# A sparse attention feeding a mixture of attention experts: one written order of 2573 operations replaced by another

## The chip, the cores and the metric

The kernel runs on one core of one Trainium2 chip. The metric is the device time of one execution in microseconds (us), from the start of the program to its end; lower is better. The profile's span runs from the first to the last instruction of the program, and is a little shorter than the time.

## What is computed

The input is `q`, `k`, `v` for 8 batches, 8 heads, 576 positions and 64 values a head, and the weights of four experts. Stage one is attention under fixed sparse masks; stage two sends its result through four causal attention experts, of which each position keeps the two with the largest gates.

```python
# stage one, a head: the first four heads see the last 32 positions, the others every 32nd
mask_local   = (rel >= 0) & (rel < 32)
mask_strided = (rel >= 0) & (pos[None, :] % 32 == pos[:, None] % 32)
x = softmax(where(mask, q @ k.T / 8, -1e9)) @ v            # heads side by side: 576 x 512
# stage two, expert e of four
logits = x @ w_gate                                        # weights w: softmax over the two largest
a  = softmax(where(causal, -1e9, (x @ wq[e]) @ (x @ wk[e]).T / 8))
ye = a @ (x @ wv[e]) @ wo[e]
out += mask[..., None] * w[:, :, kk:kk+1] * ye             # 8 x 576 x 512, float32
```

## The kernel before

The work is cut into 2573 small operations. The kernel first only notes them: `op(...)` stores what an operation does, the engine or the two engines that can do it, the tiles that it reads and writes and, for TensorE, the shape of the array that it uses (`mode`: the full 128 x 128 array, two halves of 64 rows, two of 64 columns, quarters of 64 x 64, and strips of 64 x 32 or 32 x 64). Nothing is issued until `schedule()` walks a list of numbers written into the kernel, `ORDER`, and issues the operations in that order. Each engine executes its own in the order of the list, and engines wait for each other only through the data and the buffers. So the list is the order of five queues at once: the four engines' and that of SyncE, which issues every DMA. `SECOND` names the operations that are done by the second of their two engines, and `FILL` the warming matmuls.

Buffers come from rings. The eight PSUM banks (ring `bank`, one of the tiles printed as `bank`) take every product; `nat` (3) holds `q` and `k` as loaded, `v1` (2) values, `th` (4) transposed weights, `ys` (3) output tiles. An operation that is the first to use a buffer asks its ring for one at its place in the list, and gets the free one whose last use stands furthest back in the list. In execution it then waits until that last use is over.

A fill is issued only `if o.fill and RB.first() is not None`: where no bank is free at that place of the list, none is made. Each fill is a 128 x 128 matmul of the identity into a free bank, whose result nobody reads; in float32 that is two matmul instructions.

`stage1(b, hp)` does two heads of one batch: loads (`load_qk`, `load_v`), transposes of `q` and `k` (`tp`, on TensorE in batches 0 and 1, else `tq` on VectorE), scores (`sl`, L628, for local heads, `s`, L642, for strided ones), mask, softmax over VectorE, GpSimd and ScalarE, a transpose of the weights (`pt`, L706, or on VectorE), values (`xal`, L736, or `xa`, L755), and a split of the result into a rounded part and its remainder (`xh`, `xl`). The local scores are 80 matmuls of 32 columns an operation, local values 84.

Stage two for a batch: `project` makes queries and keys of two experts at a time (`pj`, 12 matmuls, L906; for batch 0's first pair in parts of 3, L918), `values2` values and gates (`vp`, L853), `attend` the causal scores (`s2`, L992, and `s2_4`, L972), their softmax, transposes (`t2`, L1048, copied by `t2_out`), and the values (`acc`, L1081); `out_tile` makes 128 rows of output (`yp`, 6 matmuls, L1110), copies them (`yp_out`) and stores them. The copies `tp_out`, `pt_out`, `vp_out`, `t2_out` and `yp_out` can be done by ScalarE or VectorE; they share L338. `load_weights` loads the experts' weights and splits them (`hi_w`, `lo_w`).

Of the kernel before, what the change touches and what calls it, by code (L numbers as in the profile page):

```python
# [20 lines left out]
def attention_moe_kernel(  # L21
# [59 lines left out]
    class Ring:  # L81
# [24 lines left out]
        10, 11, 14, 15, 48, 52, 55, 58, 85, 86, 91, 111, 120, 121, 125, 146, 155, 159, 162, 165, 168, 171, 174,  # L106
        180, 185, 194, 197, 200, 210, 214, 215, 238, 247, 248, 249, 252, 253, 275, 310, 313, 314, 335, 336, 401,
        434, 468, 500, 501, 533, 534, 545, 566, 567, 578, 599, 632, 665, 666, 698, 722, 765, 798, 842, 855, 863,
        896, 897, 929, 963, 974, 995, 1029, 1086, 1106, 1127, 1161, 1269, 1353, 1355, 1356, 1375, 1406, 1426,
        1443, 1444, 1478, 1485, 1494, 1497, 1513, 1597, 1615, 1617, 1630, 1632, 1634, 1711, 1737, 1778, 1784,  # L110
        1802, 1836, 1852, 1855, 1877, 1920, 1924, 1974, 1990, 1992, 2038, 2097, 2119, 2122, 2123, 2126, 2142,
        2166, 2187, 2188, 2190, 2191, 2210, 2231, 2233, 2235, 2281, 2282, 2332, 2341, 2343, 2346, 2348, 2350,
        2396, 2399, 2427, 2429, 2449, 2453, 2455, 2477, 2483, 2491, 2494, 2518, 2520, 2524, 2548, 2559,
    }
    ORDER = [
        1, 0, 2, 44, 8, 45, 3, 13, 12, 5, 88, 15, 87, 56, 10, 7, 51, 6, 4, 9, 46, 49, 11, 16, 14, 18, 53, 55,
        47, 52, 57, 58, 48, 122, 54, 89, 19, 123, 21, 17, 201, 23, 202, 59, 50, 20, 25, 157, 90, 92, 22, 24,
        240, 93, 26, 27, 91, 28, 29, 61, 62, 64, 63, 65, 31, 94, 30, 96, 66, 239, 68, 127, 97, 129, 32, 67, 124,
        98, 99, 100, 128, 69, 33, 126, 40, 125, 36, 131, 213, 71, 70, 72, 203, 34, 60, 169, 132, 207, 37, 205,
        134, 208, 35, 172, 277, 215, 102, 278, 101, 41, 209, 308, 133, 135, 210, 73, 214, 307, 74, 103, 105,  # L120
        136, 104, 138, 75, 212, 38, 137, 251, 106, 252, 95, 39, 204, 76, 107, 211, 139, 206, 246, 81, 109, 83,
# [134 lines left out]
    ]  # L256
    FILL = {
        8: 4, 13: 1, 56: 2, 76: 2, 96: 6, 127: 2, 213: 1, 241: 3, 251: 8, 1131: 1, 1136: 1, 1137: 1, 1138: 5,
        1143: 1, 1144: 4, 1149: 4, 1150: 6,
    }  # L260

    def op(kind, eng, key, fn, r=(), w=(), mode=None, dmas=(), after=()):
# [931 lines left out]
```

## Time and profile before

| | us |
|---|---|
| median of 3 runs | 445.7 |
| lowest and highest run | 442.08, 446.44 |
| the profiled execution, its time | 446.46 |
| the profiled execution, its span | 444.7 |
| TensorE busy | 427.8 |
| VectorE busy | 345.9 |
| ScalarE busy | 269.5 |
| GpSimd busy | 221.0 |

The mean granted clock of TensorE over the span is 0.992 of full speed. The profile is of one execution. A page gives sums over the span; the timeline, the stretches and the chain of waits give places. The profile names engines PE (TensorE's matmuls), PEld (its weight loads, which overlap the matmuls), DVE (VectorE), ACT (ScalarE), POOL (GpSimd) and SP (SyncE). A matmul's end is modelled, so neighbouring matmuls overlap in these rows.

### The profile page before, as it was taken

The page shows a single profiled execution, that of the slowest core. Times are in us where ns is not written, and L with a number is a line of the kernel's source. Part 1 is how long each engine was busy: PE and PEld are TensorE (multiplying, and loading weights), DVE is VectorE, ACT ScalarE, POOL GpSimd, SP SyncE. Part 2 cuts the span into 40 slices and gives each one's busy share as a digit, 9 for nine tenths or more (in the row PEclk, how much of TensorE's full clock was granted, in tenths as well). Part 3 has the DMA queues.
Part 4 walks back from the last instruction along what each step waited for, and adds up shares of the span by engine and source line. Part 5 has one row for each costly group of instructions (what it writes and reads, how often), then busy time and mean ns, then how long its engine had stood idle before and what let it go on. Part 6 is the DMA issues. An engine that isn't in the chain of part 4 may idle for free.

```text
span 444.7 us, 19093 instructions
## 1 busy us (share of the span) xinstructions
PE 427.8 (96%) x7716; PEld 382.8 (86%) x7716; DVE 345.9 (78%) x1104; ACT 269.5 (61%) x848; POOL 221.0 (50%) x408
## 2 busy tenths in 40 slices
PE   7899998999989999999999999999999999999996
PEld 6788987977879998997889898998879998998874
DVE  6878899889985977789997768796998868555651
ACT  4475537676675757556486475557565577645662
POOL 4556641777534633376536552346833754405440
PEclk9989999999999999999999999999999999999999
DMA  6756656636545604545625336215832211001113
GB/s 178 188 140 151 126 116 125 125 58 107 113 103 118 124 23 105 113 90 118 117 50 131 68 59 124 61 33 107 193 76 73 67 43 54 1 1 58 45 68 118
DMA packets 156272, 41.89 MB, mean 94 GB/s; under 512 B 145976, under 2 KB 149432, under 8 KB 156184
## 3 DMA queue, kind: packets, MB, share of 16 engines
q1 hardware_dynamic: 156184, 40.67, 41.3%
q8 instruction: 61, 1.00, 0.9%
q14 instruction: 27, 0.22, 0.2%
HBM read 31.20 MB, written 9.44 MB: 91 GB/s over the span
## 4 chain that ended last, share of the span: by engine, by line
PE 85%; DVE 4%; SPq 3%; issue 3%; DMA 2%; ACT 2%; POOL 1%; POOLq 0%; DVEq 0%; ACTq 0%
PE bank L906 20%; PE bank L1110 12%; PE bank L853 10%; PE bank L1081 9%; PE bank L992 7%; PE bank L1048 6%; PE bank L736 4%; PE bank L972 3%; PE bank L755 3%; PE bank L628 3%; PE bank L642 3%; DMA v<-in_v_dram 1%; PE bank L706 1%; PE bank L816 1%; SPq L549 1%
## 5 line engine op out<-in xcount | busy, mean ns | idle before, releaser
L1029 POOL TENSOR_SCALAR p<-p,st,wt 128x512 f32<-128x512 f32 (+3 forms) x128 | 76.6, 610 | 42.4 <-DVE st L1013 17.2
L1004 ACT ACTIVATE p<-p,st 128x384 f32<-128x384 f32 (+3 forms) x128 | 71.8, 569 | 0.7 <-DVE st L999 0.6
L999 DVE CUSTOM_DVE_ANT_0 p<-bank,m_cau 128x128 f32<-128x128 f32 (+3 forms) x128 | 57.2, 481 | 6.6 <-PE bank L992 5.7
L927 ACT CAST qk<-bank 128x288 fp32r<-128x288 f32 x64 | 25.2, 400 | 56.3 <-PE bank L906 49.8
L338 ACT COPY th<-bank 128x384 f32<-128x384 f32 (+2 forms) x119 | 46.1, 436 | 13.5 <-PE bank L1048 9.8
L523 DVE STREAM_TRANSPOSE qkt<-nat 128x576 f32<-128x576 f32 x48 | 47.7, 1006 | 1.5 <-DMA nat<-in_k_dram 1.2
L1081 PE MATMUL bank<-th,vs 128*64 128x192 f32 (+4 forms) x512 | 48.5, 337 | 0.0
L1081 PEld LDWEIGHTS bank<-th,vs 128*64 128x64 f32 x512 | 33.6, 137 | 13.9 <-issue 6.9
L718 ACT CAST xh<-bank 128x128 fp32r<-128x128 f32 (+4 forms) x112 | 28.7, 322 | 21.6 <-PE bank L736 10.4
L720 DVE TENSOR_TENSOR xl<-bank,xh 128x128 fp32r<-128x128 f32 (+4 forms) x112 | 32.1, 324 | 12.4 <-ACT xh L718 11.7
L929 DVE TENSOR_TENSOR qkl<-bank,qk 128x288 fp32r<-128x288 f32 x64 | 27.8, 444 | 12.6 <-ACT qk L927 12.5
L1048 PE MATMUL bank<-ident,p 64*128 64x64 f32 x800 | 36.5, 226 | 0.5 <-DVE xl L720 0.3
L853 PE MATMUL bank<-wl_v,xh 128*128 128x260 f32 x128 | 36.2, 283 | 0.6 <-issue 0.6
L1048 PEld LDWEIGHTS bank<-ident,p 64*128 64x128 f32 x800 | 32.3, 139 | 5.3 <-issue 1.6
L853 PE MATMUL bank<-wh_v,xh 128*128 128x260 f32 x128 | 36.4, 284 | 0.0
L853 PE MATMUL bank<-wh_v,xl 128*128 128x260 f32 x128 | 36.2, 283 | 0.0
L906 PE MATMUL bank<-xh,wh_k 128*128 128x288 f32 x120 | 36.1, 301 | 0.0
L906 PE MATMUL bank<-xh,wh_q 128*128 128x288 f32 x120 | 35.9, 299 | 0.0
L906 PE MATMUL bank<-xl,wh_k 128*128 128x288 f32 x120 | 35.8, 299 | 0.0
L906 PE MATMUL bank<-xh,wl_k 128*128 128x288 f32 x120 | 35.8, 298 | 0.0
L906 PE MATMUL bank<-xl,wh_q 128*128 128x288 f32 x120 | 35.7, 298 | 0.0
L906 PE MATMUL bank<-xh,wl_q 128*128 128x288 f32 x120 | 35.5, 296 | 0.0
(182 smaller groups left out, 1254.4 us busy)
## 6 DMA issues: line engine op xcount, KB each, us to landing
out_dram<-ys SPq DMA_DIRECT2D x32, 256.0 KB
nat<-in_q_dram SPq DMA_DIRECT2D x96, 72.0 KB
nat<-in_k_dram SPq DMA_DIRECT2D x96, 72.0 KB
v<-in_v_dram SPq DMA_DIRECT2D x96, 40.0 KB
v<-in_v_dram SPq DMA_DIRECT2D x48, 54.0 KB
v<-in_v_dram SPq DMA_DIRECT2D x32, 48.0 KB
v<-in_v_dram SPq DMA_DIRECT2D x32, 45.0 KB
out_dram<-ys SPq DMA_DIRECT2D x8, 128.0 KB
```

The lines of the kernel that those rows point to most:

```text
L338: (nc.scalar.copy if e == "ACT" else nc.vector.tensor_copy)(dst, src)
L523: op("tq", {"DVE": 0.66 if local else 1.11}, k0 - 13, lambda e, x=x: nc.vector.transpose(turned(qkt.t, x), raw(x) if local else raw(x).rea ...
L720: op("xl", {"DVE": dve(n_)}, key + 0.5, lambda e, s_=s_, x_=x_: nc.vector.tensor_sub(x_(xl.t), s_(xa.t), x_(f(xh.t))), r=[xa, xh[u]], w=[x ...
L853: nc.tensor.matmul(vp.t[:, :NV], xx.t[:, t0:t0 + 128], ww.t[:, kt, :], start=i == 0, stop=i == 11)
L906: nc.tensor.matmul(pj.t[:, :HS], ww.t[:, kt, ep * 128:(ep + 1) * 128], xx.t[:, c], start=i == 0, stop=i == 11)
L992: nc.tensor.matmul(sp[a].t[:, :nk], x.t[r, 0, q0:q0 + 128], y.t[r, 1, :nk], start=i == 0, stop=i == 2)
L999: lambda e, sp=sp, p=p, a=a, nk=nk, ci=ci: nc.vector.tensor_tensor_reduce(out=p.t[:, a, :nk], in0=sp[a].t[:, :nk], in1=m_cau[:, S - nk:], ...
L1004: op("exp2", {"ACT": 0.285 + 0.00084 * nk}, k_ + 1, lambda e, p=p, a=a, ci=ci, nk=nk: nc.scalar.activation(p.t[:, a, :nk], p.t[:, a, :nk], ...
L1029: lambda e, p=p, a=a, ci=ci, t=t, nk=nk: nc.gpsimd.tensor_scalar(p.t[:, a, :nk], p.t[:, a, :nk], st.t[:, 20 + ci + a:21 + ci + a], wt.t[:, ...
L1048: nc.tensor.transpose(tp[hf].t[:, 64 * c:64 * c + 64], src, ident[r, r])
L1081: nc.tensor.matmul(acc.t[o, c0:c0 + cn], vw, th[a].t[:, s0:s0 + cn], start=j == 0, stop=j == idx[-1], skip_group_check=True)
L1110: nc.tensor.matmul(yp.t[:, :DM], xx.t[:, c0:c0 + 128], ww.t[:, ep, :], start=i == 0, stop=i == 5)
```

## The change

The three tables are replaced: `ORDER`, `SECOND` and `FILL`. The operations themselves, the rings and the tiles are the same. `ORDER` holds the same 2573 numbers in another order. `SECOND` has 165 members instead of 150, so that VectorE has 805 of the operations instead of 788, ScalarE 685 instead of 703, GpSimd 314 instead of 313; 461 on TensorE and 308 on SyncE are as before. `FILL` asks for 60 warming matmuls at 15 places instead of 52 at 17. In making the new list, an operation that asked for a buffer late was pushed behind the operation that releases it.

```diff
     SECOND = {
-        10, 11, 14, 15, 48, 52, 55, 58, 85, 86, 91, 111, 120, 121, 125, 146, 155, 159, 162, 165, 168, 171, 174,
...
+        6, 7, 10, 12, 42, 48, 49, 50, 54, 55, 86, 112, 120, 128, 146, 147, 155, 156, 168, 174, 180, 185, 188,
...
     ORDER = [
-        1, 0, 2, 44, 8, 45, 3, 13, 12, 5, 88, 15, 87, 56, 10, 7, 51, 6, 4, 9, 46, 49, 11, 16, 14, 18, 53, 55,
...
+        2553, 2554, 2560, 2555, 2556, 2564, 2565, 2557, 2570, 2566, 2567, 2571, 2568, 2572, 2569,
     ]
     FILL = {
-        8: 4, 13: 1, 56: 2, 76: 2, 96: 6, 127: 2, 213: 1, 241: 3, 251: 8, 1131: 1, 1136: 1, 1137: 1, 1138: 5,
-        1143: 1, 1144: 4, 1149: 4, 1150: 6,
+        0: 1, 13: 5, 18: 3, 33: 2, 51: 5, 92: 6, 96: 6, 131: 5, 145: 4, 241: 2, 246: 8, 1143: 3, 1144: 4, 1147:
+        1, 1149: 5,
     }
```

TensorE's own order around the first work of batch 2, written out from both lists, shows the kind of difference (operation, batch; `pt` and `s2` of earlier batches stand between):

```
before  s2 s2_4 ... xa(1) s2 sl(2) sl(2) pj(1) pj(1) vp(1) vp(1) vp(1) vp(1) pj(1)
after   sl(2) s2_4 pt s2 s2 xa(1) xa(1) sl(2) s2 s2 pj(1) pj(1) pj(1) vp(1) pj(1)
```

## Rows read from the trace of the kernel before

**Rows 1.** The page: busy us, share of the span and instructions of each engine.

```profile
PE 427.8 (96%) x7716; PEld 382.8 (86%) x7716; DVE 345.9 (78%) x1104; ACT 269.5 (61%) x848; POOL 221.0 (50%) x408
```

**Rows 2.** Stretches: from:to and length, busy us (xinstructions) by engine, clock, DMA share, GB/s.

```profile
0.00:43.30 43.30, 37.47 (x977) 33.08 (x977) 34.81 (x123) 23.91 (x64) 21.91 (x47) 0.96 0.63 164
...
72.00:80.00 8.00, 6.28 (x168) 6.03 (x150) 6.16 (x18) 4.94 (x19) 3.43 (x9) 0.79 0.66 109
80.00:440.00 360.00, 355.29 (x6058) 317.22 (x6057) 279.90 (x886) 223.19 (x708) 181.68 (x329) 1.00 0.38 82
```

**Rows 3.** Timeline of SyncE's queue, first 75 us: start us, us, line, out<-in, count.

```profile
37.56 2.23 SPq L555 DMA_DIRECT2D v<-in_v_dram  x6
...
47.16 3.82 SPq L549 DMA_DIRECT2D v<-in_v_dram  x8
```

**Rows 4.** Chain that ended last: start us, us, what (xcount of merged matmuls).

```profile
1.25 3.83 PE bank L1130 x10
5.08 0.89 PE bank L301 x8
...
34.22 1.03 PE bank L628 x59
...
43.39 0.80 PE bank L755 x40
...
143.41 1.04 PE bank L736 x57
...
264.63 0.84 PE bank L755 x41
...
315.73 2.77 PE bank L1110 x12
...
432.14 2.96 PE bank L1110 x12
```

**Rows 5.** Timeline at the holes: start, us, engine, line, count [idle before <-releaser].

```profile
74.95 0.27 PEld L628 LDWEIGHTS bank<-qkt 64*32 64x32 f32 x25 [1.88 <-issue]
...
103.08 0.20 PE L642 MATMUL bank<-qkt,nat 64*64 64x54 f32 x1 [0.40 <-issue]
...
133.72 0.43 PEld L628 LDWEIGHTS bank<-qkt 64*32 64x32 f32 x35 [1.06 <-issue]
...
215.43 0.26 PEld L628 LDWEIGHTS bank<-qkt 64*32 64x32 f32 x22 [0.96 <-issue]
...
279.46 0.19 PEld L853 LDWEIGHTS bank<-wl_v,xh 128*128 128x128 f32 x1 [0.83 <-issue]
```

**Rows 6.** Stretches between holes: the first of five and the last.

```profile
74.30:102.95 28.65, 27.31 (x509) 24.58 (x509) 24.72 (x74) 18.64 (x56) 19.88 (x36) 0.94 0.52 91
...
232.90:279.20 46.30, 45.66 (x883) 41.18 (x883) 34.79 (x115) 28.36 (x97) 22.34 (x40) 1.00 0.45 93
```

**Rows 7.** The page's DMA queues: packets, MB, share of 16 engines.

```profile
q8 instruction: 61, 1.00, 0.9%
```

**Rows 8.** Stretches ahead of two holes, and one ahead of none.

```profile
70.20:73.23 3.03, 3.03 (x162) 2.24 (x153) 2.96 (x11) 3.03 (x16) 0.45 (x2) 1.00 0.93 183
130.30:132.83 2.53, 2.53 (x160) 2.30 (x152) 2.44 (x9) 2.19 (x9) 0.00 (x0) 1.00 0.68 112
...
66.00:70.20 4.20, 4.20 (x130) 3.82 (x130) 4.06 (x22) 4.04 (x16) 0.00 (x0) 1.00 0.48 108
```

**Rows 9.** Groups by line: count | busy us, mean ns | idle before, what ended it.

```profile
L338 ACT COPY th<-bank 128x384 f32<-128x384 f32 (+2 forms) x119 | 46.1, 436 | 13.5 <-PE bank L1048 9.8 <-DVE st L999 2.5 <-ACT oh L1092 0.6
...
L338 DVE COPY th<-bank 128x256 f32<-128x256 f32 (+2 forms) x41 | 18.6, 473 | 4.2 <-PE bank L1048 3.9
...
L736 PE MATMUL bank<-pt,v 32*64 32x64 f32 (+1 forms) x1344 | 18.4, 230 | 2.6 <-DMA v<-in_v_dram 1.4 <-DVE pt L696 1.2
...
L301 PE MATMUL bank<-ident 128*128 128x128 f32 x58 | 8.6, 286 | 0.0
```

**Rows 10.** The stretch from 76 to 80 us, with the granted clock behind POOL.

```profile
76.00:80.00 4.00, 4.00 (x21) 4.00 (x21) 3.04 (x6) 1.75 (x6) 2.98 (x7) 0.60 0.67 108
```

## What I expected of the change

> **What bounds the kernel now.** I read the page's busy line first: TensorE (PE) is busy 96% of a span of 444.7 us, VectorE (DVE) 78%, ScalarE (ACT) 61%, GpSimd 50% [rows 1]. The change removes no instruction that computes, so it can only win back what TensorE idles or loses. The view by stretches says where that is [rows 2]: up to 43.3 us TensorE is busy 37.47 us, so it idles 5.8; from 72 to 80 us it idles 1.7; from 80 to 440 us 4.7. Over the whole span it idles 444.7 - 427.8 = 16.9 us, and no order saves more than that plus what a lower clock and changes of the array's shape cost.
>
> The first stretch is set by SyncE, whose queue issues one DMA after another. The values of heads 6 and 7 of batch 0 (tile `v1`) are issued from 37.56 us on, six DMAs in 2.23 us [rows 3], and the product that needs them, the last of batch 0's strided values, starts at 43.39 us [rows 4]. From there on TensorE is the bound, and its holes are of two kinds.
>
> Most are marked "issue": TensorE stands still inside a run of tiny matmuls and waits for no other engine. Six such holes behind 45 us are 1.88, 0.40, 1.06, 0.96 (twice, one shown) and 0.83 us [rows 5], together 6.09 us. Between the six lie five stretches; in the first TensorE executes 509 + 509 = 1018 matmuls and loads, in the last 883 + 883 = 1766 [rows 6]: just short of 4 x 256 = 1024 and of 7 x 256 = 1792, as the other three are of multiples of 256. What is missing, 6 to 26, fits semaphore waits, which these rows don't count. One queue named "instruction" carries 61 packets [rows 7], and TensorE's 7716 matmuls and 7716 loads [rows 1] over 61 are 253. So I read the holes as TensorE running out of code, at fixed places of its own stream: code comes some 256 instructions at a time, and the next portion isn't there yet. Ahead of two of the holes TensorE went through 315 and 312 instructions in 3.03 and 2.53 us; where no hole follows it takes 4.2 us for 260 [rows 8]. From the left edges of those two windows, 70.20 and 130.30 us, to the restarts at 74.95 and 133.72 us [rows 5] it took 4.75 and 3.42 us. So where some 290 instructions run in less than about 3.5 us, TensorE waits for the rest.
>
> The Trainium skill ("Runtime: NRT & Kernel Launch", section "Instruction fetch mechanics") says that code is refilled in blocks of 256 instructions, and that crossing a block is mostly hidden. The spacing here agrees with the block. "Hidden" does not agree with the six holes; by that sentence they would have another cause, which is the first rival below.
>
> The second kind are waits for values: 1.4 us for `v` in all [rows 9], by my reading of the lists for the second pair of heads of batch 1 and of batch 2. Then the clock: from 76 to 80 us, right behind the longest hole, the granted clock averages 0.60, so part of it is at 1.2 GHz instead of 2.4 [rows 10]. That is 4 x 0.40 = 1.6 us lost on the bound.
>
> **The change part by part.**
>
> *Order against the code holes.* I wrote out TensorE's operations in both orders, gave each its instructions from the loops (a local score operation 80 matmuls and 80 loads, a strided one 48 and 48, local values 84 and 84, strided values 44 and 44, a projection 12 and 12) and its duration from the chain (a local score 1.03 us, local values 1.04, strided values 0.84 [rows 4], the others in the same way; a tenth or two less where the next operation has the same shape), added 0.43 of a semaphore wait to each operation, and marked every 256th instruction. In the old order this puts seven portions below 3.3 us for the 290 instructions around their mark. Two are in the start, where SyncE is the bound. The other five are the five longest holes: two local scores back to back behind a causal one (2.4 us); strided values, scores, values, local scores (2.2); two local scores again (2.5); a mix of scores and values (3.1); two local scores (3.0). The sixth hole, 0.40 us, stands at 3.7. In the new order no two local scores are neighbours (four pairs before), and one portion is below 3.6: two strided values and batch 2's second local score, 3.3 us, near 75 us. Seven more lie at 3.7 to 3.9. Shifting the marks by 12 instructions either way, for waits that I can't count, changes little: at most a second portion falls below 3.5. I leave 1.2 us of holes in the new order: 0.2 to 1.4 for the tightest, some tenths elsewhere where code comes late. Gain 6.1 - 1.2 = 4.9 us; bounds 6.1 and 0.
>
> *Clock.* Without the hole at 73 us there is no pause behind which the clock would fall: gain 1.6 us; bounds 1.6 and 0.
>
> *Loads of values.* The first late load stands 15 places ahead of its use in the old list and 43 in the new; the second 3 and 6 places. But another one (batch 3, first pair) now stands one place ahead of its use, its ask right behind the release. Of the 1.4 us I take 0.9 as gained; bounds a gain and a loss of 1.4.
>
> *Array shapes.* TensorE changes the shape of its array 173 times in the new order, 152 times in the old; 16 of the 21 more are between the full array and its two row halves. Two output products behind such a change take 2.96 us and without one 2.77 us [rows 4]: 0.19 us, either for one change or for there and back. The added ones come in pairs, eight each way, so I take there and back: 21 x 0.1 = 2.1 us lost; bounds 2.1 and 21 x 0.19 = 4.0. The Trainium skill ("TensorEngine Tiling (Array Packing)", section "Key Properties") says that changing the tiling mode drains TensorE. That rule speaks against this change, and the 0.19 us agrees with it; it gives no figure.
>
> *Warming matmuls.* A fill is made only when a bank is free in the written order. Walking that rule through both lists, 29 of the 52 old ones are made (58 matmuls [rows 9]) and 47 of the 60 new ones. Each is two matmuls of 0.11 us (8 in 0.89 us [rows 4]), so 18 x 0.22 = 4.0 us more on TensorE, all ahead of the product at 43.39. There SyncE is the bound, and its queue reaches the last values with one weight load fewer ahead (four instead of five; 8 loads take 3.82 us [rows 3], so 0.5). TensorE idles 5.8 us there [rows 2]; the 1.25 us before its first instruction [rows 4] can't be used, so 4.5 us can cover the 4.0. I take 0; without the cover it is 4.0 us. The last loads of the value weights move behind two loads of batch 2 and half a pair of batch 1's values (six DMAs, some 2.9 us [rows 3]); but ahead of the first product that needs them TensorE now has 12 us of work (ten parts of projections, four whole ones, local values, two scores), so that stays hidden.
>
> *Engine choices.* Fifteen more copies of transposed weights (`t2_out`) go from ACT to DVE, 473 ns there against 436 [rows 9]: 15 x 0.473 = 7.1 us more on DVE. Six output copies go the other way; the rest, in the start, is a handful each way. DVE at 78% [rows 1] has 99 us free and hides it: 0; without that cover at most 7.1 us.
>
> *Asks.* 85 of 1287 asks for a used buffer stand directly behind the last operation on it in the list, against 14 before; for banks 50 against 9. This is a place in a list, not a time: by TensorE's own work between the last product into a bank and the next one, the tight ones (under 1 us) fall from 82 to 65. I take 0; the slower rival is the bound. The end of the list is as before.
>
> **The sum**, against the profiled execution's own 446.46 us (its span of 444.7 and 1.8 around it): - 4.9 - 1.6 - 0.9 + 2.1 = - 5.3, so 441.2 us. The median of the three runs is 445.7, 0.76 below that execution: 440.4 us.
>
> **Rivals.**
> 1. *The holes stay*: they aren't code, or fall at other marks. For it: in the new order a local score still follows strided values twice. Against it: the spacing in 256s and the dense run ahead of each. Then the clock's fall stays too, and - 0.9 + 2.1 is left: 447.7, from the median 446.9 us.
> 2. *The start gets longer*: the warming matmuls stand in front of products that a chain over DVE waits for (DVE is busy 34.81 of the first 43.3 us [rows 2]). For it: five stand ahead of the very first transposes. Against it: SyncE's late values. Full price 4.0: 444.4 us.
> 3. *Slower: TensorE waits for banks.* Each of the 41 more bank asks right behind a release waits for the copy that releases the bank. A whole copy is 0.44 us [rows 9], 18 us in all; with two thirds of it 41 x 0.29 = 12: 452 us. At 0.13 each it eats the gain, from 0.24 each on (9.8 us) the kernel is slower by over 1%. For it: the position in the list. Against it: the wider margins in TensorE's own work.
>
> **Numbers.** Chances: forecast 0.65, rival 1 0.13, rival 2 0.13, rival 3 0.09. The forecast's own range is 436.5 (no hole, all values in time, 2 us of small waits gone as well) to 443 (changes of shape at 0.15 us, the clock falling elsewhere). The whole range reaches up to rival 1, 436.5 to 447, and leaves out rival 3 and the tails. A measurement of this kernel tells about 1% from no change: 441.2 and 450.2 us. Four fifths of the forecast lie below 441.2, or 0.53 faster; its rest and rivals 1 and 2 give 0.38 the same; rival 3 gives 0.09 slower.
>
> **What would show it.** Right: behind 45 us no "issue" hole over 0.5 us but one near 75 us; no stretch there with a clock below 1; the last strided values of batch 0 at about 43 us again; TensorE idle under 2 us from 80 to 440. Wrong: holes as long as before at other places (rival 1); those values at 45 us or later (rival 2); many waits of some tenths on copies of DVE and ACT (rival 3).

## The result

The changed kernel is slower: a median of 448.6 us (20 runs, 446.05 to 452.26) against 445.6 us of the kernel before (20 runs, 442.08 to 449.9). The ratio of the runs is 1.0074, with a 95% interval of 1.0051 to 1.0096: 3.3 us more (3.0 by the medians), where 5.3 us less was forecast. Medians and ratios, here and below, are of fast runs; five slow ones, in runs 2, 5, 12 and 18 below, are left out. The profiled execution took 449.61 us, with a span of 447.9 us: 3.15 us more than that of before.

The page's busy line of the changed kernel, beside [rows 1]: TensorE is busy 6.7 us longer. The row of the warming matmuls (L301, now L302) grows from 58 instructions and 8.6 us to 94 and 13.8, so 5.2 of the 6.7 us are the 18 more warming matmuls, which the prediction had priced at 4.0.

```profile
PE 434.5 (97%) x7752; PEld 387.3 (86%) x7752; DVE 351.8 (79%) x1121; ACT 266.0 (59%) x830; POOL 221.0 (49%) x409
```

The stretches that answer to [rows 2] (from:to and length, busy us and count for PE, PEld, DVE, ACT, POOL, then clock, DMA share, GB/s):

```profile
0.00:42.50 42.50, 40.06 (x1014) 36.21 (x1015) 33.39 (x120) 24.53 (x65) 18.41 (x42) 1.00 0.70 176
72.00:80.00 8.00, 7.01 (x79) 6.34 (x80) 6.18 (x20) 5.20 (x19) 3.35 (x6) 0.57 0.55 96
80.00:440.00 360.00, 355.15 (x6048) 315.38 (x6047) 284.27 (x900) 216.52 (x686) 183.09 (x333) 1.00 0.37 81
```

The start is no longer than before, so in this execution the added warming matmuls are covered. From 72 to 80 us the granted clock is 0.57, against 0.79: the slow stretch is not gone, it is longer. From 80 us on TensorE idles 4.9 us, as before (4.7).

What TensorE waits for from 45 to 440 us, in the changed kernel (line, releaser, us in total, times, longest):

```profile
PE bank L629 <- issue: 2.1, 1, 2.1
PE bank L907 <- DVE xl L721: 1.0, 1, 1.0
PE bank L1082 <- issue: 0.9, 1, 0.9
PE bank L1082 <- DVE qkl L930: 0.9, 1, 0.9
PE bank L737 <- issue: 0.4, 1, 0.4
PE bank L1049 <- DVE p1l L657: 0.3, 1, 0.3
PE bank L1111 <- DVE th L339: 0.2, 1, 0.2
PE bank L993 <- issue: 0.2, 1, 0.2
...
```

And in the kernel before, the same view:

```profile
PE bank L628 <- issue: 3.4, 3, 1.7
PE bank L736 <- DMA v<-in_v_dram: 1.4, 2, 0.8
PE bank L642 <- issue: 1.2, 2, 0.8
PE bank L853 <- issue: 0.6, 1, 0.6
PE bank L1048 <- DVE xl L720: 0.3, 1, 0.3
```

Holes marked "issue" fall from 5.2 to 3.6 us, waits for values from 1.4 to nothing, and waits for VectorE rise from 0.3 to 2.8 (two of 0.2 us of the changed kernel are among the lines left out). The last strided values of batch 0 start at 42.25 us (43.00 before; the piece at 43.39 in [rows 4] is its later part), and from there to the end of TensorE's last product it is 401.9 us against 398.0, 3.9 more. The parts of it: issue holes - 1.6; values - 1.4; waits for VectorE + 2.5; slow clock + 1.7 (6.8 us at 1.2 GHz in place of 3.4); changes of shape + 2.5 (an estimate: 21 more changes at the 0.12 us that run 8 gives). That is + 3.7, and 0.2 is not resolved. The earlier start takes 0.75 off. The slow clock is a part of this one execution more than of the kernel: by the mean granted clock of every run it costs 2.2 us in the 20 runs of the changed kernel and 2.1 in the 103 runs of the kernel before that stand beside the experiments (an estimate: the missing share of the clock times the span).

Where the waits for VectorE come from is seen on VectorE itself. Its timeline ahead of TensorE's wait at 217.3 to 218.1 us (start, us, line, out<-in, idle before):

```profile
214.89 0.78 DVE L524 STREAM_TRANSPOSE qkt<-nat 128x576 f32<-128x576 f32 x1
215.59 0.42 DVE L930 TENSOR_TENSOR qkl<-bank,qk 128x288 fp32r<-128x288 f32 x1
216.54 1.26 DVE L524 STREAM_TRANSPOSE qkt<-nat 128x576 f32<-128x576 f32 x1 [0.54 <-DMA nat<-in_k_dram]
217.65 0.43 DVE L930 TENSOR_TENSOR qkl<-bank,qk 128x288 fp32r<-128x288 f32 x1
```

The copy `qkl` at 217.65 frees the bank that the accumulation on TensorE waits for. It stands behind a transpose of loaded keys, and this one waited 0.54 us for its landing. At 317 us it is the same: a transpose waited 0.87 us for keys at 312 us, three more of them follow from 314 us on, and behind these, at 316.99 us, comes the copy `xl` that frees the projection's bank. The groups of these transposes (count, busy, mean ns, idle before and what ended it), before and after:

```profile
L523 DVE STREAM_TRANSPOSE qkt<-nat 128x576 f32<-128x576 f32 x48 | 47.7, 1006 | 1.5 <-DMA nat<-in_k_dram 1.2 <-DMA nat<-in_q_dram 0.2
```

```profile
L524 DVE STREAM_TRANSPOSE qkt<-nat 128x576 f32<-128x576 f32 x48 | 47.3, 1005 | 7.3 <-DMA nat<-in_k_dram 3.8 <-DMA nat<-in_q_dram 1.5 <-issue 1.1
```

VectorE waits 5.3 us for landings where it waited 1.4. The prediction read VectorE's free time and the loads of values, and never this row.

### The profile page after: what moved, and what is told of

It is laid out like the page before. It is cut to its first block, busy times and chain, and to the rows that moved or that the text cites. A ratio compares the mean times of both kernels' runs of the same rounds, so it can differ in the third digit from the quotient of the medians.

```text
span 447.9 us, 19144 instructions
## 1 busy us (share of the span) xinstructions
PE 434.5 (97%) x7752; PEld 387.3 (86%) x7752; DVE 351.8 (79%) x1121; ACT 266.0 (59%) x830; POOL 221.0 (49%) x409
## 4 chain that ended last, share of the span: by engine, by line
PE 78%; DVE 7%; DMA 3%; issue 2%; ACT 2%; SPq 2%; POOL 1%; DVEq 0%; ACTq 0%; POOLq 0%
PE bank L907 17%; PE bank L854 10%; PE bank L1111 10%; PE bank L1082 8%; PE bank L993 8%; PE bank L1049 6%; PE bank L737 4%; PE bank L756 3%; PE bank L629 3%; PE bank L643 3%; PE bank L973 2%; DVE qkt L524 2%; DMA nat<-in_k_dram 2%; PE bank L919 2%; SPq L496 2%
## 5 line engine op out<-in xcount | busy, mean ns | idle before, releaser
L1030 POOL TENSOR_SCALAR p<-p,st,wt 128x256 f32<-128x256 f32 (+3 forms) x128 | 76.9, 616 | 42.2 <-DVE st L1014 37.2
L1005 ACT ACTIVATE p<-p,st 128x128 f32<-128x128 f32 (+3 forms) x128 | 72.0, 565 | 8.8 <-DVE st L1000 8.8
L1000 DVE CUSTOM_DVE_ANT_0 p<-bank,m_cau 128x256 f32<-128x256 f32 (+3 forms) x128 | 57.7, 481 | 5.2 <-PE bank L993 4.3
L339 ACT COPY th<-bank 128x256 f32<-128x256 f32 (+2 forms) x104 | 40.8, 435 | 14.1 <-PE bank L1049 12.8
L721 DVE TENSOR_TENSOR xl<-bank,xh 128x128 fp32r<-128x128 f32 (+4 forms) x112 | 32.5, 324 | 10.5 <-ACT xh L719 9.1
L670 POOL TENSOR_TENSOR p1s<-p1s,st 128x648 f32<-128x648 f32 (+1 forms) x18 | 20.8, 1160 | 26.5 <-DVE st L668 23.9
```

Source lines behind the costliest of these rows:

```text
L339: (nc.scalar.copy if e == "ACT" else nc.vector.tensor_copy)(dst, src)
L721: op("xl", {"DVE": dve(n_)}, key + 0.5, lambda e, s_=s_, x_=x_: nc.vector.tensor_sub(x_(xl.t), s_(xa.t), x_(f(xh.t))), r=[xa, xh[u]], w=[x ...
L1000: lambda e, sp=sp, p=p, a=a, nk=nk, ci=ci: nc.vector.tensor_tensor_reduce(out=p.t[:, a, :nk], in0=sp[a].t[:, :nk], in1=m_cau[:, S - nk:], ...
L1005: op("exp2", {"ACT": 0.285 + 0.00084 * nk}, k_ + 1, lambda e, p=p, a=a, ci=ci, nk=nk: nc.scalar.activation(p.t[:, a, :nk], p.t[:, a, :nk], ...
L1030: lambda e, p=p, a=a, ci=ci, t=t, nk=nk: nc.gpsimd.tensor_scalar(p.t[:, a, :nk], p.t[:, a, :nk], st.t[:, 20 + ci + a:21 + ci + a], wt.t[:, ...
```

## The experiments

Each ratio is to the kernel before on the same chip; the chips differ from experiment to experiment. Runs 7 and 8 are single executions with work added, and have no line here. "Rest" is the time in the profiled execution from the start of the last strided values of batch 0 to the end of TensorE's last product.

| kernel | median us | ratio (95%) | rest us |
|---|---|---|---|
| before | 445.6 | | 398.0 |
| changed | 448.6 | 1.0074 (1.0051 to 1.0096) | 401.9 |
| 1. changed, 64 instructions ahead | 461.9 | 1.0377 (1.0334 to 1.0421) | 406.5 |
| 2. before, 64 instructions ahead | 455.6 | 1.0227 (1.0196 to 1.0258) | 398.6 |
| 3. before, five holes split | 445.6 | 0.9998 (0.9967 to 1.0029) | 398.7 |
| 4. changed, hole at 71 us split | 450.9 | 1.0111 (1.0065 to 1.0157) | 402.5 |
| 5. changed, two banks freed first | 446.9 | 1.0044 (1.0013 to 1.0075) | 399.4 |
| 6. changed, all four moves | 446.9 | 1.0048 (1.0017 to 1.0079) | 397.4 |
| 9. new order, old engines | 466.8 | 1.0481 (1.0446 to 1.0515) | 413.6 |
| 10. old order, new engines | 462.5 | 1.0353 (1.0293 to 1.0412) | 410.7 |
| 11. before, no loads | 444.9 | 0.9956 (0.9924 to 0.9988) | 393.6 |
| 12. changed, no loads | 439.4 | 0.9838 (0.9787 to 0.9890) | 391.2 |
| 13. changed, no landing wait on VectorE | 441.2 | 0.9870 (0.9820 to 0.9920) | 393.7 |
| 14. before, no landing wait on VectorE | 445.5 | 0.9965 (0.9927 to 1.0002) | 396.6 |
| 15. changed, no loads of values | 443.6 | 0.9932 (0.9891 to 0.9973) | 394.1 |
| 16. changed, four moves and early loads | 443.1 | 0.9894 (0.9841 to 0.9948) | 397.8 |
| 17. changed, early loads alone | 443.4 | 0.9961 (0.9933 to 0.9989) | 395.9 |
| 18. before, early loads | 445.6 | 0.9973 (0.9946 to 1.0000) | 396.6 |

### 1 and 2. The 256 marks moved by 64 instructions

```diff
-        for _ in range(5):
-            nc.tensor.matmul(wb.t[:, :256], ones[:, :128], ones, start=True, stop=True)
+        for _ in range(21):
+            nc.tensor.matmul(wb.t[:, :24], ones[:, :128], ones[:, :24], start=True, stop=True)
```

In the changed kernel:

> The changed kernel, its order, buffers and engine choices untouched; only the warming operation is cut finer, 21 matmuls of 24 columns (504) in place of 5 of 256 (1280), which puts 64 more matmuls and loads in front of everything and so moves every 256th instruction of TensorE 64 instructions forward in the order. Theory A (the holes are TensorE running out of code, at every 256th instruction, where the work around is dense): the holes of the changed kernel at 68, 71, 201 and 278 us go or change their place, and others appear where local scores stand at the new marks; by the same sum over the list as in the prediction, the missing time goes from 0.6 to 6.7 us, so the time rises by about 5 us, to some 453 us. Theory B (the holes belong to operations, not to places in the instruction stream): the holes stay at the same operations and the time stays within 1 us of the changed kernel's 448.6 us.

In the kernel before:

> The kernel before with the same finer warming operation, 64 instructions more ahead of everything. Theory A (code by 256 instructions): its holes move to other operations, but its list has about as many dense places at the new marks (6.9 us missing by the sum over the list, 7.4 us after the shift), so the time stays within 1 us of 445.6 us while the places change. Theory B (holes belong to operations): places and time stay. What both share is the price of the finer warming itself, 776 columns fewer and 16 matmuls more in the first microseconds, which should be nothing since SyncE sets the end of that stretch.

The edit had a price that I had put at nothing. The finer warming lasts 9.15 us instead of 3.83 [rows 4], and the eight warming matmuls behind it take twice their time (in [rows 4] 0.89 us in the chain; 1.05 in the timeline):

```profile
1.25 9.15 PE L1130 MATMUL bank<-p1l 128*128 128x24 f32 x42 [1.25 <-DVE p1l L346]
10.23 2.06 PE L301 MATMUL bank<-ident 128*128 128x128 f32 x8
```

Everything starts some 9 us later, so the medians say nothing of the holes. Behind the last strided values of batch 0 the holes marked "issue" come to 6.3 us in the new order, where they were 3.6 (+ 6.1 expected of the list), and to 6.6 in the old one, where they were 5.2 (+ 0.5 expected). The rest, + 4.6 and + 0.7 us, holds other things too: in the new order TensorE's waits for VectorE went from 2.8 to 5.1 us. The holes moved to other operations, as places in the instruction stream do. The new order has few of them only with the marks where they are.

### 3. The old order with its five longest holes split

```diff
-        ... 745, 778, 719, ...
+        ... 745, 719, ...
...
+        ... 1643, 778, 1652, ...
```

One of the five moves is shown; the others are 382 behind 1243, 613 behind 1425, 910 behind 1993, and 1783 ahead of 844.

> The kernel before with five local moves in the written order and nothing else: at each of the five longest holes (73, 133, 215, 232 and 279 us) one dense operation changes places with the one to three operations behind it (a local score behind an output product, behind a projection, behind two others; an output product ahead of a score), so that no two dense operations stand at a 256 mark. Theory A (the holes are code that comes late, and the term of the prediction was right in its mechanism): the five holes of 4.9 us in all shrink to under 1 us, the clock does not fall at 76 us, eight more changes of shape cost 0.8 us, and the time falls by 3.5 to 5 us, to about 441 us. Theory B (TensorE would have waited for something else there anyway, so that a hole removed comes back as another wait): the holes go, but the time stays within 1.5 us of 445.4 us.

TensorE's waits from 45 to 440 us in this kernel:

```profile
PE bank L1041 <- DVE xl L713: 1.9, 2, 1.1
PE bank L729 <- DMA v<-in_v_dram: 1.7, 1, 1.7
PE bank L985 <- DVE qkl L922: 0.5, 1, 0.5
PE bank L635 <- issue: 0.2, 1, 0.2
```

The five holes are gone, 5.2 us of "issue" down to 0.2, and the time is the same to within 1.5 us. In the profiled execution other waits stand in their place: 1.7 us for values at 63 us (ahead of all five moves, so not caused by them; 0.8 before), 1.9 and 0.5 for VectorE, and 6.8 us of slow clock from 65.8 us, behind the wait for values. The slow clock is not this execution's alone: it costs 3.2 us in the mean of the 12 runs, against 1.7 in the 29 runs of the kernel before beside them. Holes can be taken out by local moves; here that was not worth their length.

### 4 to 6. The changed kernel mended

Run 4 moves the second local score of batch 2 away from the two strided values ahead of it; run 5 moves two copies of VectorE ahead of transposes; run 6 does both and moves a local score behind two accumulations (910 behind 1837).

```diff
-        ... 238, 382, 1224, ...
+        ... 1217, 382, 334, ...
```

> The changed kernel with one operation moved: batch 2's second local score, which stood between two strided values and the next operations at 69 to 73 us, goes behind a causal score some operations later, so that no two dense operations follow one another at the marks of portions 11 and 12. Theory A (the 2.1 us hole at 71 us is code that comes late twice in a row, and the clock falls behind the hole for 6.8 us): the hole shrinks below 1 us, the clock falls for a shorter time or not at all, and the time falls by 2 to 4 us, to 445 to 447 us. Theory B (hole and clock have another cause, or the loss is waits elsewhere): no change, 448.6 us within 0.7.

```diff
-        ... 836, 841, 689, 749, 1648, 840, ...
+        ... 836, 1648, 841, 689, 749, 840, ...
...
-        ... 1999, 1104, 2029, 1038, ...
+        ... 1999, 891, 1104, 2029, 1038, ...
```

> The changed kernel with two VectorE operations moved in the written order and nothing else: the copy qkl that frees the bank for the accumulation at 218 us goes ahead of the transpose of loaded queries and keys that waits for a DMA at 216.5 us, and the copy xl that frees the bank for the projection at 317 us goes ahead of the three transposes that stand in front of it from 314 us on. Theory A (these two waits of TensorE, 0.89 and 1.03 us, are banks that VectorE frees late because it stands behind transposes, and are lost for good): both waits go and the time falls by 1.5 to 2 us, to about 446.8 us. Theory B (what is saved comes back at the next wait): the two waits go, but the time falls by less than 0.7 us.

> The changed kernel with the two moves of the run before, the local score of batch 2 moved behind a causal score (the hole at 71 us), and the local score of batch 6 moved behind two accumulations (the hole of 0.9 us at 277 us). Theory A (code holes, clock and late banks make the loss): without 2.1 + 0.9 us of holes, 1.9 us of late banks and most of 3.4 us that the slow clock of 6.8 us cost, the time falls by 4 to 7 us, to 442 to 445 us. Theory B (the loss is in the new order as a whole, in changes of shape and in many small waits): it falls by less than 2 us.

Each did at its place what was expected. In run 4 the hole at 71 us is gone and the clock does not fall there; in runs 5 and 6 the waits at 218 and 317 us are gone; in run 6 also the hole at 277 us. Yet run 4 gained nothing, run 5 some 1.3 us by the ratios and run 6 no more than run 5 (its theory A had 4 to 7). In all three executions another wait stands at 92 us, where the strided scores of batch 2 need loaded queries by way of VectorE and GpSimd (2.0, 1.9 and 1.1 us; in the changed kernel's own profile no wait over 0.15 us stands there). Run 4's row on VectorE shows the source:

```profile
L516 DVE STREAM_TRANSPOSE qkt<-nat 128x576 f32<-128x576 f32 x48 | 47.5, 1007 | 12.7 <-DMA nat<-in_k_dram 8.7 <-PE bank L621 2.5 <-DMA nat<-in_q_dram 1.5
```

VectorE waited 10.2 us for landings there. So the theory that the loss is two banks, two holes and a slow clock fell: that is where it shows in one execution.

### 7 and 8. The price of a change of shape, and the pace of the code

Run 7 is a probe behind the whole kernel, run 8 one inside the projections.

```diff
+    op("micro", {"PE": 60.0}, 1e6, micro, w=mu, mode=M128)
```

> The kernel before with a probe behind everything, on TensorE alone, whose output nothing reads: 24 full products of 128 columns and then 24 pairs of transposes on the array's row halves, the same operations taken in turn (48 changes of shape), then 24 full products and 24 blocks of eight tiny matmuls in the shape of the local scores, these in turn as well, and last 640 tiny matmuls in one run (1280 instructions, five portions of code) at a time when no other engine and no transfer of the kernel has anything to do. Theory A (a change of the array's shape costs about 0.1 us): the runs in turn are 4 to 6 us longer than the grouped ones, 0.08 to 0.13 us per change. Rival: a change costs 0.19 us, 9 us in all; or nothing, and the two output products of 2.96 and 2.77 us differ for another reason. For the code: if it is delivered a portion at a time at a pace of its own, the last run stops every 256 instructions, for longer than once in the kernel, and the distance of the stops gives the pace without other traffic; if the holes come from competition with the kernel's transfers, it runs through.

```diff
+                if u == 0 and ep == 0:
+                    nc.tensor.transpose(pj.t[:, 448:512], ident[:64, :], ident[:64, :64])
+                elif u == 0:
+                    nc.tensor.transpose(pj.t[:, 320:448], ident, ident)
+                nc.tensor.transpose(pj.t[:, 320:448], ident, ident)
```

> The kernel before with probes behind the projections, whose results nothing reads: every projection gets one more full transposition of 128 columns; ahead of it, the first half of each projection of the first pair gets a transposition on a row half (a change of shape there and back, inside one operation), that of the second pair a second full one, and the other halves nothing. From the last product of the projection to the added full transposition: theory A (0.1 us per change, as the prediction took): the row half adds about 0.23 us to the bare distance, the full one 0.06; rival 1 (0.16 us per change, as the alternating probe at the end of the kernel gave): about 0.36; rival 2 (a lone change is hidden by the pipeline): no more than the full one.

Grouped, the 24 full products take 5.45 us and the 24 pairs on row halves 1.66; in turn, the same work takes 14.99: 7.88 us for 48 changes, 0.164 each. Inside the projections the distance from the last product to the added transposition is 0.134 us bare (30 of them), 0.241 with a full one between (16), 0.428 with the row half (14). Of the 0.294 that the row half adds, 0.03 to 0.05 is its own work (0.035 each in the grouped probe, half of a full one's 0.107 at most), so a change costs 0.12 to 0.13. The prediction's 0.1 was low: 21 changes cost 2.5 to 3.4 us. The runs of tiny matmuls in the score's shape fell partly into a slow clock, and say nothing of this price.

The last part, 640 tiny products in 1280 matmuls, in the timeline (start, us, count, idle before):

```profile
500.95 1.55 PE L1167 MATMUL bank<-ident 64*32 64x32 f32 x128 [1.92 <-issue]
504.42 1.55 PE L1167 MATMUL bank<-ident 64*32 64x32 f32 x128 [1.92 <-issue]
507.89 1.55 PE L1167 MATMUL bank<-ident 64*32 64x32 f32 x128 [1.92 <-issue]
511.64 1.55 PE L1167 MATMUL bank<-ident 64*32 64x32 f32 x128 [2.19 <-issue]
```

And one stretch of it, with the clock and the DMA share behind POOL's busy time:

```profile
500.00:510.00 10.00, 4.65 (x384) 4.25 (x384) 0.00 (x0) 0.00 (x0) 0.00 (x0) 0.50 0.02 5
```

TensorE stops behind every 128 matmuls and 128 loads, for 1.9 to 2.2 us, with the DMA engines all but idle. TensorE ran at 1.2 GHz in this part. So the holes are code, 256 instructions a portion, and a portion takes some 3.5 us from stop to stop here without any competing load. The traces' records of the queue "instruction" [rows 7] say it directly: each portion is one packet of 16,384 bytes, and at all 66 holes of over 0.5 us that are marked "issue" and stand behind 45 us in the twenty traces, TensorE starts again 1.2 to 1.6 us after such a packet has ended. The Trainium skill ("Runtime: NRT & Kernel Launch", section "Instruction fetch mechanics") says that crossing a block is mostly hidden; the trace agrees only where a block's work takes longer than that.

### 9 and 10. Orders and engine choices crossed

Run 9 is the changed kernel with the old `SECOND`, run 10 the kernel before with the new one.

```diff
     SECOND = {
-        10, 11, 14, 15, 48, 52, 55, 58, 85, 86, 91, 111, 120, 121, 125, 146, 155, 159, 162, 165, 168, 171, 174,
...
```

102 operations go into this table and 87 out of it, so 189 change engine; the prediction had counted what is left over of that by kind.

> The changed kernel's order and fills with the engine choices of the kernel before (all copies back on their old engine: the 15 t2_out copies on ScalarE, six output copies on VectorE, and the handful in the start). Theory A (the engine choices cost nothing, the loss is code, clock and shape changes): the time stays within 1 us of 448.6 us. Theory B (VectorE, with 7.1 us more work, hands banks and operands over late, which is seen as waits of some tenths at 115, 123, 218 and 317 us): these waits go and the time falls by 2 to 3 us, to about 446 us. A third case: the new order was timed for the new choices, and with the old ones other waits appear, 450 us or more.

> The kernel before, its order and fills, with the engine choices of the changed kernel (15 more t2_out copies on VectorE, six output copies on ScalarE, the handful in the start). With the new order under the old choices (466.8 us measured) this fills the table of order against choices. Theory A (an order and its choices fit each other: copies stand in each engine's queue where their operands come just in time, so that either pair taken apart loses): 450 us or more, with many waits of TensorE for VectorE. Theory B (the choices of the changed kernel are simply the better ones, whatever the order): 445.5 us or less. By the prediction's step on engine choices (hidden by VectorE's free time): within 1 us of 445.5.

Taken apart, either pair loses 16 to 18 us. In both, TensorE's waits for VectorE and ScalarE are spread over the kernel (in run 9 nine of 0.5 to 1.2 us), and VectorE is busy no more than 75% in run 9. What the new choices cost or give with the new order, the two runs can't say. They do say that VectorE's spare time, the reason that I gave for a price of nothing, is no reason: an order holds only for the choices it was made with.

### 11 and 12. Without the loads of batches 2 to 7

```diff
         def load_qk(src, x, h, y):
+            if b > 1:
+                return
...
         def load_v(e, h):
+            if b > 1:
+                return
```

> The kernel before without the loads of queries, keys and values of batches 2 to 7: the transposes and products read what batches 0 and 1 left in the buffers, so the values computed for these batches are not the reference's; all else is done as before (and one buffer is cleared on GpSimd at the start). SyncE's queue has only the weights, the first two batches and the stores, and VectorE never waits for a landing. Theory A (up to some 95 us TensorE's pace is that of the loads, and a hole there costs nothing; behind it the old order seldom waits for a load): 1 to 3 us less than before, with the code holes where they were. Theory B (loads never bind behind 45 us): within 0.7 us of before.

> The changed kernel without the same loads (batches 2 to 7 compute on old data, as in the run beside it). Theory A (the new order's gain on code holes is eaten by VectorE standing behind transposes that wait for loads, with banks asked for directly behind the copies that queue there): the waits at 115, 218 and 317 us go, the time falls by 4 us or more, and the changed kernel comes out at or below the kernel before treated alike. Theory B (the loss is in what TensorE itself does, changes of shape and the hole at 71 us with the slow clock behind it): it falls by no more than the other, and stays some 3 us above it.

TensorE's waits from 45 us to the end, the kernel before and then the changed one:

```profile
PE bank L634 <- issue: 3.8, 4, 1.7
PE bank L761 <- issue: 1.5, 2, 0.8
PE bank L1054 <- DVE xl L726: 0.4, 1, 0.4
PE bank L978 <- ACT th L338: 0.3, 1, 0.3
```

```profile
PE bank L635 <- issue: 1.3, 1, 1.3
PE bank L1117 <- DVE th L339: 0.2, 1, 0.2
PE bank L1055 <- POOL p L1036: 0.2, 1, 0.2
```

This is the kernel that the prediction described. One hole of 1.3 us is left, where the list had the tight place, against 5.3 us in the old order; no wait for a bank is longer than 0.2 us; the clock does not fall between 45 us and TensorE's last product in either. The changed kernel is 5.4 us faster than the other treated alike (439.4 against 444.9), and the loads cost it 9.2 us, the old order 0.7 by the medians and 2.0 by the ratio. Of the 5.4 us some 1.5 are the clock, which in the mean of the runs costs 2.5 us in the old order and 1.0 in the new one: without the loads the prediction's step on the clock comes out. In these two executions half of the difference is the start (40.45 against 43.08 us) and 2.4 us the rest. The start of the new order varies: 40.9 to 44.7 us in the four executions that have it unchanged (the changed kernel and runs 4 to 6), where the old order's is 42.6 to 43.1 (the kernel before, runs 3, 7 and 14).

### 13 to 15. By which way the loads cost

Runs 13 and 14 keep all loads and let VectorE's transposes read a weight tile that has long been there:

```diff
-                    turned(qkt.t, x), raw(x) if local else raw(x).rearrange("p (g d) -> p g d", d=32)),
+                    turned(qkt.t, x), old() if local else old().rearrange("p (g d) -> p g d", d=32)),
```

Run 15 leaves out the loads of values alone (the second half of the edit of run 12).

> The changed kernel with all loads, but VectorE's transposes of queries and keys of batches 2 to 7 read a weight tile that has long been there in place of the loaded tile, so VectorE never waits for a landing (what these batches compute is not the reference's). Traffic and SyncE's issues stay; for heads 4 to 7 GpSimd still waits for the landing. Theory A (the changed kernel's loss with loads comes through VectorE: it stands behind transposes that wait for a landing, the copies behind them free banks late): most of the 9 us that leaving out the loads gave comes back, 440 to 443 us. Theory B (the loads cost it through SyncE's queue, late values and late code, not through VectorE): the time falls by less than 3 us.

> The kernel before treated alike (transposes of batches 2 to 7 on a weight tile). Without the loads it came out 1.5 to 2 us faster. Theory A: as much or less here, 444 to 446 us, since its banks are seldom asked for directly behind the copy that frees them. Theory B: the same as the changed kernel's fall.

> The changed kernel without the loads of values of batches 2 to 7 alone (their products work on old data); queries and keys are loaded and waited for as before, with SyncE's queue shorter by 144 and more DMAs. Theory A (VectorE behind landings): little, 446 to 448 us, as far as queries and keys are issued earlier with fewer values ahead of them on SyncE. Theory B (SyncE's queue and the values): 441 us or less.

TensorE's waits in run 13 from 45 to 440 us:

```profile
PE bank L632 <- issue: 2.1, 1, 2.1
PE bank L1085 <- issue: 0.6, 1, 0.6
PE bank L1114 <- DVE th L339: 0.2, 1, 0.2
...
```

With all traffic in place, taking VectorE's wait for landings away gives 7.4 of the 9.2 us by the medians, 9 of 10.5 by the ratios. The edit takes one more thing away. In the changed kernel SyncE's queue waits for these transposes to free the buffers of the loaded tiles,

```profile
SPq L496 <- DVE qkt L524: 13.4, 3, 7.6
```

and in run 13 it does not. But the loads are issued no earlier for it: set against TensorE's own progress in the two traces, the 192 loads of batches 2 to 7 start 0.0 us apart in the mean (median 0.2 us later in run 13). So it is VectorE's waits that the gain comes from. The wait at 217 us and that at 317 are gone. The hole at 71 us stays at 2.1 us, but here the clock does not fall behind it. The old order gains 1.6 us by the ratio from the same edit, its interval reaching to none, and 0.1 by the medians. Run 15 gains 5 to 6 us as well. There the values' issues are out of SyncE's queue, and the row of VectorE's transposes shows the same wait shrunk:

```profile
L524 DVE STREAM_TRANSPOSE qkt<-nat 128x576 f32<-128x576 f32 x48 | 47.0, 1004 | 3.8 <-issue 1.6 <-DMA nat<-in_q_dram 1.2 <-PE bank L631 0.9
```

Theory A had put that at 0.6 to 2.6 us: SyncE's queue counts for more than I thought, though its way also goes by VectorE. How much of run 15's gain has to do with values themselves stays open.

### 16 to 18. Loads put earlier, nothing left out

In the written order each load of queries or keys that stands less than 45 places ahead of its transpose moves forward to that distance, or to right behind the ask for its buffer. Keys of batch 5, for instance, stood directly ahead of their transpose (841):

```diff
-        ... 678, 654, 1647, 1681, 836, 841, ...
+        ... 678, 654, 1647, 1681, 841, ...
```

> The changed kernel with the four moves of the mended one, and 33 loads of queries and keys moved forward in the written order so that the last stands 45 places ahead of its transpose (or directly behind the ask for its buffer); nothing is left out. Theory A: VectorE's waits for landings shrink from 7 us and more to under 2, TensorE's waits for VectorE go, 441 to 444 us, below both kernels. Theory B (SyncE's queue is full where it matters, so that loads put ahead push values or other loads back): no gain, 446 to 449 us.

> The changed kernel with the 33 loads of queries and keys moved forward, and none of the four other moves; nothing is left out. Theory A (VectorE's waits for landings are the main part of the loss): most of the gain of the run with both (ratio 0.989) is here already, a ratio of 0.99 to 0.995 and 441 to 444 us. Theory B (the two copies and two scores moved by hand made that gain): 447 us or more.

> The kernel before with its loads moved forward by the same rule (54 of them). Theory A (the old order has the code holes as its bound and VectorE waits only 1.4 us for landings): within 1.5 us of the kernel before, at most as much gained as the 1.6 us that taking the wait away gave. Theory B (earlier loads help any order alike): 4 us faster.

TensorE's longest waits in run 17, from 45 to 440 us:

```profile
PE bank L749 <- DMA v<-in_v_dram: 0.8, 1, 0.8
PE bank L900 <- DVE xl L714: 0.8, 1, 0.8
PE bank L1075 <- issue: 0.7, 1, 0.7
PE bank L636 <- DMA nat<-in_q_dram: 0.7, 1, 0.7
...
```

The 33 loads alone turn 1.0074 into 0.9961, 5 us, and the changed kernel is then faster than the one before. Its ratio misses the 0.99 to 0.995 of theory A, and theory B's 447 us is refuted. Run 16 is 3.0 us below run 17 by the ratios and 0.3 by the medians, on another chip, so what the four other moves add stays open. VectorE's waits for landings fall less than expected, from 5.3 to 3.7 us in run 17 (4.3 in run 16; under 2 expected). Nor does run 17's gain come by them alone. In the profiled execution the rest falls by 6.0 us: 1.7 are TensorE's waits for VectorE, 2.7 code holes and 3.4 the slow clock, and new waits for landed values and queries take 1.9 back. Over all runs the clock's part is 1.0 (2.2 to 1.3 us). The old order gains 1.2 us by the same rule, its interval reaching to none. Treated alike in this way, with nothing left out, the new order leads the old one by only 0.5 us by the ratios and 2.2 by the medians.

## Why the prediction was wrong

*What bounds the kernel: code holes.* Right in the mechanism: probe, moved marks, packets of code and runs 11 and 12 show it. Its size was read too high: the 6.1 us count the idle time ahead of weight loads, and ahead of the matmuls the same holes come to 5.2. The term of - 4.9 us is - 4.0 without the loads (5.3 to 1.3) and - 1.6 with them. The tight place near 75 us was named, but its hole is 2.1 us, above the 0.2 to 1.4 given: its packet of code runs from 70.28 to 71.57 us, TensorE stood still from 70.9 us on, and the portion before had come late as well, with a stop of 0.2 us at 68 us. That the one made the other late fits, but no run shows it; the sum treated each portion alone. Two holes of 0.4 and 0.9 us stand where "some tenths" did.

*Clock.* - 1.6 came out as + 1.7 in the profiled execution and as about nothing in the mean of the runs (2.2 us against 2.1). The step took it that the fall belongs to the old hole at 73 us. The new hole at 71 us brought one of twice the length. That a stop brings a fall is not certain either way: 2.1 us at 71 us did in the changed kernel and did not in run 13.

*Loads of values.* - 0.9 was taken and - 1.4 measured, within the bounds.

*Changes of shape.* + 2.1 at 0.1 us each; at 0.12 to 0.16 it is 2.5 to 3.4. The Trainium skill ("TensorEngine Tiling (Array Packing)", section "Key Properties") says that a change drains the array. Runs 7 and 8 agree in so far as a change costs 0.12 to 0.16 us; the draining itself no run shows.

*Warming matmuls.* Right as far as four executions tell: the last strided values start at 40.9 to 44.7 us, around the old 43, with no sign of the 4 us of rival 2.

*Engine choices.* Runs 9 and 10 can't give the pair's own price; they show that VectorE's free time, the reason given for the zero, hides nothing by itself.

*Asks.* This is the step that failed. It weighed each ask against TensorE's own work between two products, and took 0. What counts is what stands ahead of the copy that frees the bank, on that copy's engine: VectorE runs its list in order, transposes of loaded queries and keys are in it, and where a landing is late the copy behind it is late too. With banks asked for right behind their release there is nothing to absorb that. The loads of queries and keys were never looked at, though a row of before gives VectorE's wait for them (1.4 us). Rival 3 had the place and the sign; its price was put on all 41 asks alike, 0.29 us each, where two of about 1 us, four small ones and what hangs on them did it. Run 13 prices the whole way at 7.4 us. Between the two profiled executions the rest falls by 8.1: 2.6 are TensorE's waits for VectorE, 3.4 the slow clock (1.2 in the mean of the runs), 0.7 code holes, and 1.4 is not resolved.

So a gain of 4 to 5 us was there (runs 12 and 13 against 11 and 14), and a term of + 7 to + 9 us for loaded queries and keys was missing. Run 13 shows that it goes by VectorE's waits, and run 15 that SyncE's queue has a part in how late the landings are. Why the clock falls behind one stop and not behind another stays open.

## What to carry to other kernels

Where an order pushes asks for a buffer right behind its release, look at the engine that releases: every operation ahead of the releasing one that waits for a transfer is now on the path. Read the waits of the helper engines for landings, not only their busy share, and give each load a lead over its first reader before tightening anything else. A hole on the bounding engine is worth its length only if the next value, bank or landing is ready earlier.

## What the runs showed of the hardware

- A run of tiny matmuls stops behind every 256 instructions of TensorE for 1.9 to 2.2 us, also with a DMA share of 0.02; stop to stop it is 3.5 to 3.75 us (run 7, at a granted clock of 0.50).
- At all 66 holes of over 0.5 us marked "issue", TensorE started again 1.2 to 1.6 us after the end of a packet of 16,384 bytes on the queue "instruction".
- In run 7's probe TensorE stopped from 466.7 to 468.6 us, worked, and stopped again at 469.9; at 469.8 us the granted clock fell to 1.2 GHz and stayed there to the end of the span, 62 us, while TensorE worked and stopped in turn.
- Eight warming matmuls of 128 columns took 2.06 us behind forty-two of 24 columns (9.15 us of work), and 1.05 us behind ten of 256 columns (3.83 us).
- A change of the array's shape between the full array and a row half costs 0.12 to 0.16 us (runs 7 and 8).
